# An attention recurrence and two MoE layers on one core: where the first weights are decoded, and in which order the first two units start

## The chip, the cores and the metric

The kernel runs on one core of one Trainium2 chip. The metric is device time in microseconds (us) of one execution; each timed number is the median of several runs. The core has five engines with queues of their own, each working its queue in order: TensorE (PE; PEld is its weight load), VectorE (DVE), ScalarE (ACT), GpSimd (POOL), and SyncE (SP), which here issues all DMAs.

## The reference

Attention with a complex decay, then two layers on its output. What is computed, cut to what matters:

```python
scale = np.minimum(mag, 0.999) / (mag + 1e-06)          # mag = |a|
a_re_n, a_im_n = a_re * scale, a_im * scale
for t in range(S):                                      # per batch, head: S is D x D
    S_re, S_im = ar * S_re - ai * S_im + k_t v_t, ar * S_im + ai * S_re
    y[:, :, t] = q_t @ S_re
x = y.transpose(0, 2, 1, 3).reshape(B * S, H * D)
x = (silu(x @ w_gate) * (x @ w_val)) @ w_out
h = x @ w_in
return (h - np.tanh(h)) @ w2_out
```

Four batches, 8 heads, 768 positions, head size 48: 3072 tokens of 384 values. The first layer has 1536 inner columns, the second 2048. The weights come as float64, q, k, v and a as float32.

## The kernel before

**Attention.** A unit is 128 positions of one batch, all heads (24 units); a group is two units. `group_steps` makes the decay's weights for a group: normalise a (`squares`, `norm_root`, `norm`), transpose it on TensorE and copy it into `PL` (`put_a`), then 14 cumulative complex products on VectorE (`cstep`: one product of 128x384 into `prod`, L266, and two sums back into `PL`, L268 and L269), seven along e and seven along b. Between the products of group 0 stands the normalisation of group 1. Then `PL` is copied to `NW` (L312, L313), its inverse is made (two squares L345 and L346, root L348, square L349, products L347, L350, L351), and the factors over the unit's length go out to `lam_d` and come back as `LS`. `PL` has one buffer, so group 1's copies wait for group 0's `NW`.

`unit_a` transposes a unit's q and k (`psQ`), multiplies with the weights to `QK` (L370, L371, L376), writes `QK` to HBM and reads it back with heads apart as `TK` and `TQ` (L378, L383), and transposes k's part (`psK`). `unit_b` makes scores (`psS`, L420), masks them, makes the state `Z` (`psG`), its shifted copy `Zs` through a DMA, and on GpSimd `Hn` from the earlier state (L413 to L415); then the output `psY`, its copy `y` (L450), and the transposed token block `x` in two parts, cast and residual (L463, L464). `QK`, `TK`, `Kn` and `Z` have one buffer, `TQ` has two. `window(b, a)` interleaves the steps of one unit's `unit_b` with the next one's `unit_a`.

**MoE 1.** `moe1_tile` works on 2 or 3 units of tokens (`TILES`). For each of 12 blocks of inner columns it makes 18 matmuls (`l`, L554), Silu on ScalarE (L558), the gated product on VectorE (L563), a split into cast and residual (L514, L515) and nine matmuls with the output weights (`acc`, L538). Between these steps `bg` draws steps of attention for later tiles. MoE 2 follows after the last tile.

**Decode.** A weight block arrives as raw 64-bit words. `words` makes a float32 of it in one pass on ScalarE (L140) and four on VectorE (L141 to L144); `decode` splits it into a cast (L150) and a residual, the latter on TensorE (L158 to L160) if `by_pe`, or on VectorE (L152). `dec1_jobs` is a list of 24: the gate and value columns of blocks 0 to 7 ("gv", 128x768), then in turn an output block ("o", 128x384) and a gate and value block. `raw` has two buffers, and `dec1` loads the next block only behind the decode that frees a buffer. `dec1(3)` is called while group 0 is made; `dec1(N_PRE + 2)`, up to the tenth job, after the code of units 0 and 1, and `bg` in the first tile makes the rest.

**Order.** The kernel is written as these streams, and a scheduler then puts the instructions into each engine's queue: in the order of the code by priority, with later code moved ahead where an engine would wait by its own reckoning. `tc.issue_after(ins)` makes the instructions in its block, on the engine of `ins`, stand behind `ins`; it is no wait.

Of the kernel before, what the change touches and what calls it, by code (L numbers as in the profile page):

```python
# [13 lines left out]
ALU = mybir.AluOpType  # L14
# [27 lines left out]
def tile_kernel(ctx: ExitStack, tc: tile.TileContext, q, k, v, a_re, a_im, w_gate, w_val, w_out, w2_in, w2_out, out):  # L42
    nc = tc.nc
    PE, ACT, DVE, POOL, SP = nc.tensor, nc.scalar, nc.vector, nc.gpsimd, nc.sync
# [17 lines left out]
    N_PRE, QAT, QDEP = 8, 15, 4  # L62
# [121 lines left out]
    def dec1(n, by_pe=False):  # L184
        while prog["dec"] < min(n, len(dec1_jobs)):
            kind, f = dec1_jobs[prog["dec"]]
            r = raws[prog["dec"]]
            prog["dec"] += 1
            t = raw_p.tile([P, 2 * DM], F32, tag="dt", name="dt", bufs=2)
            if kind == "o":  # L190

                w = m1.tile([P, 2, DM], F32R, tag="wo", name="wo", bufs=3)
                wo_t[f] = w
                decode(r[:, 0], w[:, 0], w[:, 1], t[:, 0:DM])
                SP.dma_start(out=wo_d[f], in_=w.bitcast(F32))
            else:
                decode(r.rearrange("p a c -> p (a c)"), *wgv[f], t, by_pe)
            dec1_load()
# [18 lines left out]
    def load_qkv(u):  # L217
        if u < NU:
            for nm, src in (("q", q), ("k", k), ("v", v)):
                t = a2.tile([P, DM], F32, tag=nm, name=nm)  # L220
                SP.dma_start(out=heads(t), in_=nat(src, u))
                st[nm, u] = t

    def squares(eng):
        ar, ai = st["a"]
        s1, s2 = T("s1"), T("s2")
        ACT.activation(out=s1, in_=ar, func=AF.Square)
        ACT.activation(out=s2, in_=ai, func=AF.Square)
        eng.tensor_tensor(out=s1, in0=s1, in1=s2, op=ALU.add)
        st["sq"] = s1, s2  # L230
# [31 lines left out]
    def cstep(prev, cur, n):  # L262

        sh = [P, 2] + list(cur.shape[1:])
        pr = a2.tile(sh, F32, tag="prod", name="prod", bufs=1)
        DVE.tensor_tensor(out=pr, in0=prev.unsqueeze(2).to_broadcast(sh), in1=cur.unsqueeze(1).to_broadcast(sh), op=ALU.mult)  # L266
        cv, pv = cur.rearrange("p (n c) r -> p n c r", n=n), pr.rearrange("p i (n c) r -> p i n c r", n=n)
        DVE.tensor_tensor(out=cv[:, :, 0], in0=pv[:, 0, :, 0], in1=pv[:, 1, :, 1], op=ALU.subtract)  # L268
        DVE.tensor_tensor(out=cv[:, :, 1], in0=pv[:, 0, :, 1], in1=pv[:, 1, :, 0], op=ALU.add)  # L269

    def group_steps(g0):
        grp = list(range(g0, g0 + G))
# [24 lines left out]
                yield  # L297
        rows = PL.rearrange("p e c b g j h -> p (e c) b (g j h)")
        for b in range(1, 8):
            cstep(rows[:, 14:16, b - 1], rows[:, :, b], 8)  # L300
            yield
            if g0 == 0 and b == NA0:
                squares(DVE)
                norm_root(G)
                yield
                norm(DVE)
                yield
# [157 lines left out]
        yield  # L465

    def window(b, a):

        b = unit_b(b) if b is not None else iter(())
        a = unit_a(a) if a is not None else iter(())  # L470

        for s_ in (a, b, b, a, a, b, a, b, a, b):
            if next(s_, 0) is None:
                yield
        for s_ in (b, a):
            for _ in s_:
                yield
# [180 lines left out]
    prog = {"done": -1, "n": 0, "dec": 0, "credit": 0.0, "group": 0, "unit": -1, "more": 0.0}  # L658
# [23 lines left out]
    while prog["done"] < TILES[0] - 1:  # L682
        att_next(TILES[0] - 1, SHARE0)
        if prog["n"] == QAT:

            dec1(QDEP - 1, True)
            for u in range(2):
                with tc.issue_after(raw_ins[QDEP]):
                    load_qkv(u)
    dec1(N_PRE + 2, True)  # L690
    banks[:] = [(ps_a, "at")]
    second = ExitStack()
    w2_hl, w2 = [], []
# [64 lines left out]
    with tc.If(bad > 0):  # L758
        with ExitStack() as gen:
# [12 lines left out]
            with tc.For_i(0, q.shape[2], TB) as t0:  # L772
# [24 lines left out]
                for t in range(TB):  # L797
                    rows = [x[:, t, :].unsqueeze(2).to_broadcast(full) for x in (ar, ai, qq, kk)]
# [102 lines left out]
```

## Time and profile before

| what | us |
|---|---|
| median of 3 runs (lowest to highest) | 1247.72 (1244.65 to 1250.12) |
| the profiled execution | 1244.15 |
| its span, first to last instruction | 1242.4 |
| TensorE busy, share of the span | 1131.6, 91% |
| VectorE busy | 989.9, 80% |
| ScalarE busy | 693.9, 56% |
| start of the first tile's first matmul | 129.9 |

The profile is of one execution. A line of its timeline says when an instruction started and how long it took, which line of the kernel it comes from, and, in brackets, how long its engine had been idle and what ended that. Matmul ends are modelled, so a busy TensorE is not at its peak. The granted clock is the share of full speed that TensorE was given: 0.5 is 1.2 GHz, 1.0 is 2.4 GHz.

### The profile page before, as it was taken

To read this page: it belongs to the slowest core of one execution; us is meant where nothing else is said; L and a number is where in the kernel's file an instruction comes from. 1 tells how busy PE (TensorE), PEld (TensorE's weight loads), DVE (VectorE), ACT (ScalarE), POOL (GpSimd) and SP (SyncE) were. 2 spreads that over 40 slices of the span, in tenths; PEclk is the share of its full clock that TensorE was granted. 3 is DMA by queue.
4 is the path that set the end of the run, shared out by engine and by line. 5 is a ranking of instruction groups with operands and counts; after the bars stand their busy time and mean duration, and the time that the engine had idled before them with its cause. 6 is when DMAs were issued, how large, how long until landed. Compare 5 with 4: busy or idle time off the path is not lost.

```text
span 1242.4 us, 20766 instructions
## 1 busy us (share of the span) xinstructions
PE 1131.6 (91%) x7512; PEld 1100.3 (89%) x7512; DVE 989.9 (80%) x2255; ACT 693.9 (56%) x1454; POOL 124.2 (10%) x108
## 2 busy tenths in 40 slices
PE   4337898999899999999999999989999999999997
PEld 2116898999899899999999999988999999999997
DVE  6988897797796859687684428899898898898986
ACT  6463847657556363746535225566666656566664
POOL 0002241231120102122011000000000000000000
PEclk9656899999999999999999999989999999999999
DMA  6585668688777687768755538860110101101000
GB/s 172 145 194 160 160 194 192 170 205 199 179 184 193 163 204 175 167 140 196 181 139 137 164 97 258 264 206 33 58 33 26 58 1 58 39 20 58 1 20 22
DMA packets 282286, 163.50 MB, mean 132 GB/s; under 512 B 155328, under 2 KB 263232, under 8 KB 282176
## 3 DMA queue, kind: packets, MB, share of 16 engines
q1 hardware_dynamic: 282176, 162.10, 50.3%
q8 instruction: 61, 1.00, 0.3%
q14 instruction: 49, 0.40, 0.1%
HBM read 121.26 MB, written 37.86 MB: 128 GB/s over the span
## 4 chain that ended last, share of the span: by engine, by line
PE 62%; DVE 15%; ACT 12%; DMA 8%; issue 2%; SPq 1%; ACTq 0%; DVEq 0%
PE l L635 15%; PE l L617 15%; PE l L554 15%; PE acc L538 7%; PE psS L420 3%; DMA TQ<-qk_d 2%; DVE prod L266 2%; DMA qk_d<-QK 1%; DVE PL L268 1%; ACT NW L313 1%; PE psY L448 1%; DVE lo L515 1%; PE psY L446 1%; DVE QK L376 1%; DMA raw<-in_moe_w_val_dram 1%
## 5 line engine op out<-in xcount | busy, mean ns | idle before, releaser
L554 PE MATMUL l<-x,wgv 128*128 128x256 f32 (+1 forms) x2160 | 361.4, 313 | 11.6 <-ACT t L558 7.5
L554 PEld LDWEIGHTS l<-x,wgv 128*128 128x128 f32 x2160 | 320.6, 194 | 14.9 <-ACT t L558 8.7
L635 PE MATMUL l<-x,wi 128*128 128x384 f32 x1152 | 223.1, 338 | 6.3 <-DVE t L584 5.7
L635 PEld LDWEIGHTS l<-x,wi 128*128 128x128 f32 x1152 | 202.4, 189 | 8.4 <-DVE t L584 7.4
L514 ACT CAST hi<-t 128x384 fp32r<-128x384 f32 (+1 forms) x248 | 119.0, 480 | 154.0 <-DVE t L563 125.3
L617 PE MATMUL l<-w,hi 128*128 128x384 f32 x768 | 178.4, 338 | 0.0
L538 PE MATMUL acc<-hi,wo 128*128 128x256 f32 (+1 forms) x720 | 175.8, 309 | 0.6 <-DMA wo<-wo_d 0.6
L515 DVE TENSOR_TENSOR lo<-t,hi 128x384 fp32r<-128x384 f32 (+1 forms) x248 | 138.0, 556 | 32.2 <-ACT hi L514 31.8
L617 PEld LDWEIGHTS l<-w,hi 128*128 128x128 f32 x768 | 139.1, 189 | 0.0
L577 ACT ACTIVATE t<-l 128x384 f32<-128x384 f32 x128 | 63.4, 496 | 125.1 <-PE l L635 110.0
L538 PEld LDWEIGHTS acc<-hi,wo 128*128 128x128 f32 x720 | 125.0, 191 | 0.9 <-issue 0.8
L538 PE MATMUL acc<-lo,wo 128*128 128x256 f32 (+1 forms) x360 | 109.6, 310 | 1.8 <-DVE lo L515 1.6
L617 PE MATMUL l<-w,lo 128*128 128x384 f32 x384 | 110.4, 337 | 0.0
L563 DVE TENSOR_TENSOR t<-t,l 128x256 f32<-128x256 f32 (+1 forms) x120 | 56.2, 469 | 60.0 <-PE l L554 43.4
L266 DVE TENSOR_TENSOR prod<-PL 128x384 f32<-128x384 f32 x168 | 100.1, 596 | 2.9
L579 DVE TENSOR_TENSOR l<-l,t 128x384 f32<-128x384 f32 x128 | 72.2, 564 | 35.4 <-ACT uu L578 34.3
L558 ACT ACTIVATE t<-l 128x256 f32<-128x256 f32 (+1 forms) x120 | 51.6, 430 | 63.0 <-PE l L554 62.3
L580 ACT ACTIVATE vv<-uu,gbias 128x384 f32<-128x384 f32 x128 | 80.0, 625 | 2.8
L420 PE MATMUL psS<-TQ,TK 96*128 96x128 f32 x384 | 55.9, 296 | 27.1 <-DMA TQ<-qk_d 25.7
L420 PEld LDWEIGHTS psS<-TQ,TK 96*128 96x128 f32 x384 | 52.1, 209 | 29.0 <-issue 21.8
L584 DVE COPY_PREDICATED t<-far,l 128x384 f32<-128x384 int32 x128 | 75.7, 592 | 2.5
L538 PEld LDWEIGHTS acc<-lo,wo 128*128 128x128 f32 x360 | 68.7, 191 | 2.7 <-DVE lo L515 2.7
(130 smaller groups left out, 1856.4 us busy)
## 6 DMA issues: line engine op xcount, KB each, us to landing
wo<-wo_d SPq DMA_DIRECT2D x108, 384.0 KB, 3.9
qk_d<-QK SPq DMA_DIRECT2D x24, 768.0 KB, 4.7
raw<-in_moe_w_out_dram SPq DMA_DIRECT2D x28, 384.0 KB, 3.3
TK<-qk_d SPq DMA_DIRECT2D x48, 192.0 KB, 4.0
TQ<-qk_d SPq DMA_DIRECT2D x48, 192.0 KB, 5.0
x<-o_d SPq DMA_DIRECT2D x16, 576.0 KB, 5.2
raw<-in_moe_w_in_dram SPq DMA_DIRECT2D x16, 384.0 KB, 4.1
ar<-in_a_re_dram SPq DMA_DIRECT2D x24, 192.0 KB, 4.1
```

The costliest lines, as they stand in the source:

```text
L266: DVE.tensor_tensor(out=pr, in0=prev.unsqueeze(2).to_broadcast(sh), in1=cur.unsqueeze(1).to_broadcast(sh), op=ALU.mult)
L420: PE.matmul(ps[:, P * i:P * (i + 1)], lhsT=TK[:, 4 * hh + i], rhs=TQ[:, 4 * hh + i], start=True, stop=True)
L514: ACT.copy(out=hi, in_=t)
L515: DVE.tensor_tensor(out=lo, in0=t, in1=hi.bitcast(F32), op=ALU.subtract)
L538: PE.matmul(acc[j], lhsT=w[:, a, j * P:(j + 1) * P], rhs=m[b], start=(f == 0 and i == 0), stop=(f == NF1 - 1 and i == 2))
L554: PE.matmul(p, lhsT=w[a][:, kk], rhs=x[b][:, kk, 0:n_t], start=(n == 0), stop=(n == 3 * NJ - 1))
L577: ACT.activation(out=t, in_=p, func=AF.Tanh)
L579: DVE.tensor_tensor(out=p, in0=p, in1=t, op=ALU.subtract)
L580: ACT.activation(out=vv, in_=uu, func=AF.Square, scale=1.0 / G_C, bias=gbias)
L584: DVE.copy_predicated(out=t, mask=far, data=p)
L617: PE.matmul(acc[tb], lhsT=g[a][:, tb * P:(tb + 1) * P], rhs=w2_hl[f][:, b], start=(f == 0 and n == 0), stop=(f == NF2 - 1 and n == 2))
L635: PE.matmul(p, lhsT=wi_hl[a][:, kk, sl], rhs=x[b][:, kk, :], start=(n == 0), stop=(n == 3 * NJ - 1))
```

## The change

Two things are changed. The decode of jobs 3 to 9 (called by `dec1(N_PRE + 2, True)`) is put into a block `issue_after` on the last sum of group 0's last product, kept in `prog["cs"]`: on VectorE none of its passes may stand ahead of that sum. And `window`, for the pair of unit 0's `unit_b` and unit 1's `unit_a`, takes three steps of unit 1 first (queries, keys, `QK` and its DMAs), then five of unit 0, then the last two of unit 1.

```diff
@@ cstep
-        DVE.tensor_tensor(out=cv[:, :, 1], in0=pv[:, 0, :, 1], in1=pv[:, 1, :, 0], op=ALU.add)
+        return DVE.tensor_tensor(out=cv[:, :, 1], in0=pv[:, 0, :, 1], in1=pv[:, 1, :, 0], op=ALU.add)
@@ group_steps
         for b in range(1, 8):
-            cstep(rows[:, 14:16, b - 1], rows[:, :, b], 8)
+            cs = cstep(rows[:, 14:16, b - 1], rows[:, :, b], 8)
+            if g0 == 0:
+                prog["cs"] = cs.ins
@@ window
+        first = a == 1
...
-        for s_ in (a, b, b, a, a, b, a, b, a, b):
+        for s_ in (a, a, a, b, b, b, b, b, a, a) if first else (a, b, b, a, a, b, a, b, a, b):
@@ main
-    dec1(N_PRE + 2, True)
+
+    with tc.issue_after(prog["cs"]):
+        dec1(N_PRE + 2, True)
```

Line numbers behind the first edit grow by two, and by up to five towards the end: L383 becomes L385, L558 becomes L561. The queues change as follows. In the names, `dt_687`, `dt_705`, `dt_723`, `dt_741` are the decodes of blocks 3 to 6, `dt_954` is block 9's, `dt_776`, `dt_886` and `dt_1048` are those of output blocks 0 to 2; `raw_738` is block 7's raw weights, `raw_756` output block 0's, `raw_803` block 9's.

VectorE before, in the later half of group 0's products, with group 1's normalisation (L248 to L250):

```order
L266 TENSOR_TENSOR prod_330<-PL_160 128x384
L248 TENSOR_TENSOR s1_245<-s1_245,s2_246 128x768
L141 TENSOR_SCALAR dt_723<-dt_723 128x768
L268 TENSOR_TENSOR PL_160<-prod_330 128x8x12
L269 TENSOR_TENSOR PL_160<-prod_330 128x8x12
L249 SCALAR_TENSOR_TENSOR ai_208<-ai_208,sgn_69,s1_245 128x768
L250 TENSOR_TENSOR ar_205<-ar_205,s1_245 128x768
L142 TENSOR_SCALAR dt_723<-dt_723 128x768
L266 TENSOR_TENSOR prod_334<-PL_160 128x384
L141 TENSOR_SCALAR dt_741<-dt_741 128x768
L143 SCALAR_TENSOR_TENSOR dt_723<-raw_702,dt_723 128x768
```

VectorE now, from the last but one of group 0's products on:

```order
L266 TENSOR_TENSOR prod_342<-PL_160 128x384
L268 TENSOR_TENSOR PL_160<-prod_342 128x8x12
L269 TENSOR_TENSOR PL_160<-prod_342 128x8x12
L266 TENSOR_TENSOR prod_346<-PL_160 128x384
L268 TENSOR_TENSOR PL_160<-prod_346 128x8x12
L269 TENSOR_TENSOR PL_160<-prod_346 128x8x12
L141 TENSOR_SCALAR dt_687<-dt_687 128x768
L141 TENSOR_SCALAR dt_705<-dt_705 128x768
```

The decodes of blocks 4 to 6 no longer stand between the products; those of blocks 3 and 4 begin behind the last sum, and the others later still.

SyncE before, from unit 0's `QK` to its `TQ` and the store behind it:

```order
L378 DMA qk_d_85<-QK_414 128x12x128
L177 DMA raw_896<-in_moe_w_out_dram 128x384
L221 DMA q_662<-in_q_dram 128x8x48
L383 DMA TK_418<-qk_d_85 48x8x128 x2
L383 DMA TQ_419<-qk_d_85 48x8x128 x2
L195 DMA wo_d_83<-wo_887 128x768
```

SyncE now, from unit 0's `QK` to unit 1's `TK`:

```order
L380 DMA qk_d_85<-QK_414 128x12x128
L221 DMA q_662<-in_q_dram 128x8x48
L221 DMA k_664<-in_k_dram 128x8x48
L180 DMA raw_738<-in_moe_w_gate_dram 128x3x128
L385 DMA TK_418<-qk_d_85 48x8x128 x2
L385 DMA TQ_419<-qk_d_85 48x8x128 x2
L180 DMA raw_738<-in_moe_w_val_dram 128x3x128
L380 DMA qk_d_85<-QK_482 128x12x128
L177 DMA raw_756<-in_moe_w_out_dram 128x384
L385 DMA TQ_487<-qk_d_85 48x8x128 x2
L385 DMA TK_486<-qk_d_85 48x8x128 x2
```

A load of raw weights (block 7) now stands ahead of unit 0's `TK`, and unit 1's `QK` and `TQ` follow unit 0's directly, with its `TK`, which waits for the one buffer, last.

ScalarE before, ahead of the first Silu (`t_816`):

```order
L348 ACTIVATE x2_840<-NW_682,tiny_78 128x768
L259 COPY PL_1125<-psA_1157 128x3x8x8 x2
L260 COPY A0_1126<-psA_1157 128x3
L349 ACTIVATE x2_840,chk_82<-x2_840 128x768
L558 ACT_TABLE_LOAD
L558 ACTIVATE t_816<-l1_806 128x256
```

ScalarE now, at the same place:

```order
L140 ACTIVATE dt_954<-raw_803 128x768
L348 ACTIVATE x2_840<-NW_682 128x768
L259 COPY PL_1125<-psA_1127 128x3x8x8 x2
L260 COPY A0_1126<-psA_1127 128x3
L140 ACTIVATE dt_1048<-raw_896 128x384
L561 ACT_TABLE_LOAD
L561 ACTIVATE t_816<-l1_806 128x256
L259 COPY PL_1125<-psA_1157 128x3x8x8 x2
L260 COPY A0_1126<-psA_1157 128x3
L350 ACT_TABLE_LOAD
L350 ACTIVATE x2_840<-NW_682,tiny_78 128x768
L561 ACT_TABLE_LOAD
L561 ACTIVATE t_952<-l1_942 128x256
```

The first passes of block 9 and of output block 2 stand ahead of the first Silu, and group 1's root (L350, before L348) behind it, with a table load on either side.

## Rows read from the trace of the kernel before

**Rows 1.** Windows: stretch, length; busy PE, PEld, DVE, ACT, POOL; clock; DMA, GB/s.

```profile
0.00:129.90 129.90, 61.07 (x230) 42.52 (x230) 104.03 (x222) 68.15 (x129) 12.70 (x21) 0.69 0.64 164
...
129.90:261.20 131.30, 121.46 (x989) 119.24 (x987) 109.39 (x267) 83.98 (x180) 34.94 (x25) 0.96 0.77 190
...
160.00:180.00 20.00, 17.77 (x145) 17.59 (x144) 20.00 (x44) 7.66 (x17) 12.60 (x6) 0.91 0.73 203
```

**Rows 2.** Timeline (start, length in us, engine, line): group 0's last sum.

```profile
58.31 0.25 DVE L269 TENSOR_TENSOR PL<-prod 128x96 f32<-128x96 f32 x1
```

**Rows 3.** Timeline, from group 0's products to unit 0's QK.

```profile
62.00 0.89 ACT L313 COPY NW<-PL 128x384 f32<-128x384 f32 x1
...
67.27 0.83 ACT L259 COPY PL<-psA 128x192 f32<-128x192 f32 x2 [0.32 <-PE psA L256]
...
79.91 0.95 DVE L376 TENSOR_TENSOR QK<-qk,NW 128x768 f32<-128x768 f32 x1
```

**Rows 4.** Timeline, unit 0's QK through HBM to its scores.

```profile
80.89 0.37 SPq L378 DMA_DIRECT2D qk_d<-QK  x1
...
86.23 1.16 SPq L383 DMA_DIRECT2D TQ<-qk_d  x2
...
93.13 3.75 PE L420 MATMUL psS<-TQ,TK 96*128 96x128 f32 x16 [11.01 <-DMA TQ<-qk_d]
```

**Rows 5.** Timeline, unit 0's output, unit 1, the first gated product.

```profile
98.39 1.95 PE L446 MATMUL psY<-v,SC 128*128 128x48 f32 x16
...
102.45 1.59 DVE L376 TENSOR_TENSOR QK<-qk,NW 128x768 f32<-128x768 f32 x1
...
114.38 3.76 PE L420 MATMUL psS<-TQ,TK 96*128 96x128 f32 x16 [5.38 <-DMA TQ<-qk_d]
...
127.34 0.46 ACT L450 COPY y<-psY 128x384 f32<-128x384 f32 x1
...
132.17 1.28 ACT L558 ACT_TABLE_LOAD   x1
...
135.31 0.41 DVE L563 TENSOR_TENSOR t<-t,l 128x256 f32<-128x256 f32 x1
```

**Rows 6.** Timeline, two first decode passes; DMA issues, median us to landing.

```profile
43.25 0.90 ACT L140 ACTIVATE dt<-raw 128x768 f32<-128x768 f32 x1 [0.72 <-DMA raw<-in_moe_w_val_dram]
...
117.01 0.92 ACT L140 ACTIVATE dt<-raw 128x768 f32<-128x768 f32 x1
...
raw<-in_moe_w_val_dram SPq DMA_DIRECT2D x12, 384.0 KB, 4.9
```

**Rows 7.** VectorE's groups up to 129.9 us: busy us, mean ns | idle.

```profile
L144 DVE SCALAR_TENSOR_TENSOR dt<-raw,dt 128x768 int32<-128x768 int32 x12 | 11.4, 949 | 0.1
...
L141 DVE TENSOR_SCALAR dt<-dt 128x768 f32<-128x768 f32 x12 | 6.8, 564 | 7.3 <-ACT dt L140 7.3
...
L144 DVE SCALAR_TENSOR_TENSOR dt<-raw,dt 128x384 int32<-128x384 int32 x5 | 2.7, 549 | 0.0
...
L141 DVE TENSOR_SCALAR dt<-dt 128x384 f32<-128x384 f32 x5 | 1.8, 355 | 4.1 <-ACT dt L140 4.1
```

**Rows 8.** VectorE's waits from 129.9 to 261.2 us: total, times, longest.

```profile
DVE t L563 <- PE l L554: 6.7, 6, 2.7
DVE NW L347 <- ACT x L346: 3.4, 2, 2.3
```

**Rows 9.** Timeline, last output block's decode; the second tile's fifth gated product.

```profile
193.31 1.06 DVE L152 TENSOR_TENSOR wo<-dt,wo 128x384 fp32r<-128x384 f32 x1 [2.05 <-ACT wo L150]
...
217.31 0.41 DVE L563 TENSOR_TENSOR t<-t,l 128x256 f32<-128x256 f32 x1
```

**Rows 10.** Timeline, GpSimd beside VectorE.

```profile
98.57 2.10 POOL L250 TENSOR_TENSOR ar<-ar,s 128x768 f32<-128x768 f32 x1
...
98.93 1.85 DVE L268 TENSOR_TENSOR PL<-prod 128x96 f32<-128x96 f32 x1
...
163.29 6.32 POOL L414 TENSOR_TENSOR Zs<-Zs,LS 96x384 f32<-96x384 f32 x1 [8.91 <-DMA Zs<-Z]
```

## The prediction

> **What bounds the kernel now.** I read the stages first. Up to 129.9 us, where the first matmul of the first MoE tile starts, TensorE is busy for less than half of the time at a mean granted clock of 0.69; VectorE is busy for 104.03 us. In the next two tiles TensorE is busy for 121.46 of 131.3 us [rows 1]. So the start is a chain of waits, and from there on time is TensorE's. A start that ends earlier reaches the end as it is, unless the two tiles behind it become longer. The forecast is the sum of these two.
>
> The chain of the start, in order of time: group 0's cumulative products on VectorE, which end at 58.56 [rows 2]; the rest of that group's weights, and unit 0's QK, whose second pass ends at 80.86 [rows 3]; QK through HBM into TK and TQ, and unit 0's scores at 93.13 [rows 4]; unit 1's QK at 104.04, its scores at 114.38, its y at 127.34, the load of Silu's table at 132.17 and the first gated product (L563) at 135.31 [rows 5]. I take that product as the end of the start, since TensorE's third block can't be written before it frees a bank.
>
> **Term 1: group 0's products.** Before, the decodes of blocks 4, 5 and 6 stand among them (block 3's was done ahead of them). One decode is two passes of 0.56 us and two of 0.95 [rows 7], 3.0 us, or 2.7 since neighbours overlap by some 0.09. Three are 8.0 us; I take 0.5 off for gaps between products that they filled. Group 0 ends at 58.56 - 7.5 = 51.0. The price: block 5's raw weights can be loaded only when block 3's last pass has freed their buffer, and that pass now stands behind the products, with block 4's between its passes: four long ones, four short ones and the group's small joins put it at 57.6.
>
> **Term 2: unit 0's QK.** ScalarE has four copies and two squares to make, at 0.78 us a piece (a copy is 0.89 long and overlaps its successor [rows 3]): 51.0 to 55.7. Then its order puts two sets of evictions of group 1 (0.83 and a small copy each [rows 3]) ahead of the root, and block 3's cast and half a set ahead of the root's square, which ends at 61.5. Two VectorE passes of 0.95 end at 63.3. The cast and copies ahead of qk's second half end at 65.6, and two QK passes at 67.5. Before it was 80.86: 13.3 us earlier.
>
> **Term 3: the scores.** On SyncE the load of block 7 now stands ahead of TK, and it waits for block 5's decode. That one's own load is issued by 61.6 and takes 4.9 us to land [rows 6]; its passes, between qk and products, end at 72.9. QK has landed by then: it is issued at 80.89 and read by 86.23 at the latest [rows 4], so 67.5 + 5.3. TK and TQ go out from 73.4, TQ at 74.5, and from TQ's issue to the scores it took 6.9 us [rows 4]: 81.4. TensorE has block 6's products ahead of the scores until 82.0. Unit 0's scores: 82.0 against 93.13. Unit 1's QK no longer stands behind them: its transposes follow unit 0's, and it ends at 75.5 against 104.04 [rows 5]. But TK has one buffer. Unit 1's TK waits for unit 0's last score, 82.0 + 3.8 [rows 4], and lands some 5 us later: scores at 91 against 114.38. That is the reordering's gain at its largest, 23 us.
>
> **Term 4: from there to the first gated product.** Some is handed back. Between unit 1's scores and its y TensorE now has block 7's decode, group 2's first transposes and the state's product. Half of unit 1's output, 16 matmuls, takes 1.95 us at the rate of 98.39 [rows 5] and twice that at the lower clock (0.69 on average over the start): y at 102 to 110 against 127.34. What decides then is a load. ScalarE has the first decode pass of an output block ahead of the first Silu; that block's load stands on SyncE behind block 9's, which waits for block 8's last pass at 108 to 113.5 (block 8's own load stood behind that of v, which unit 0's output freed at 94). Load 4.9, two first passes and two sets of evictions 3.5, table 1.28 [rows 5], Silu 0.4: the first gated product at 118 to 124. I take 121.5. **At the start: 135.3 - 121.5 = 13.8 us gained.**
>
> **Term 5: what is put off.** Ahead of the first gated product VectorE has 28 instructions fewer: 12 long ones of decode (four of 0.56, eight of 0.95 with three residuals), 12 short ones (five of 0.35, seven of 0.55), and two long passes (0.95) and two halves of qk (0.35) of group and unit. By the durations [rows 7] that is 18.1 us, and 15.7 without the overlaps. At the third tile's first gated product both orders have done the same work. So these two tiles carry 15.7 us more on VectorE: 109.39 + 15.7 = 125.1. Of its idle 21.9 us, 6.7 are waits for TensorE [rows 8], which a fuller engine need not make; the other twelve lines of waits, from the 3.4 us for ScalarE's squares down [rows 8], are 12.5 together and stay. 125.1 + 12.5 = 137.6 against 131.3: **6.3 us handed back**, between 0 (all idle time is filled) and 15.7 (none is). Two further table loads, since Silu and the root alternate at the tile's start, are 2.6 us of ScalarE, counted at nothing: it is busy for 83.98 of 131.3 us [rows 1]. Without that cover they cost 2.6.
>
> **Sum.** -13.8 + 6.3 = -7.5 us. The profiled execution took 1244.15 us (span 1242.4), which gives 1236.6; it lies 3.6 under the median of the runs, 1247.72. Against the median: 1240.2. What the measurement can tell from no change is about 0.5%, 6.2 us.
>
> **Rivals.** *Hidden whole.* VectorE fills its idle time, which is 21.9 us against the 15.7 put off, and the start alone counts: 13.8 us, or up to 17 with the full clock in term 4: 1231 to 1234. Against it: from 160 to 180 VectorE has no idle time at all [rows 1], and this is where blocks 9 to 11 now fall.
>
> *All handed back.* VectorE and GpSimd shut each other out: a 128x96 pass, 0.25 elsewhere, took 1.85 us while GpSimd had a product running, and one of GpSimd's took 6.32 us beside a full VectorE [rows 10]. Then VectorE's idle time beside GpSimd's 34.94 us [rows 1] isn't free, nothing fits in, and all of term 5 comes back: -13.8 + 15.7 = +1.9, 1249.6. The Trainium skill, "SBUF — State Buffer", section "SBUF: two separate sides", says that the port pair which the two share is an exclusive lock, held for an instruction, while the other blocks; by that rule the time would be this rival's. The trace agrees on the lock, with the 1.85 us, but in the 6.32 us it was GpSimd that was kept out, so deferred passes can also push GpSimd's work aside.
>
> *Decode too slow, and the kernel slower.* The raw weights have two buffers, so blocks go in rounds of two: load, first pass, three passes, next load. Before, one buffer's first passes start at 43.25 and, five rounds later, at 117.01 [rows 6]: 14.8 us a round. In the first tile seven output blocks end within 45.3 us, the last residual starting at 193.31 [rows 9]: 15.1 us for two. Now some twelve blocks, six rounds, are left behind the first gated product. TensorE's order needs the last ahead of the second tile's sixth block, about at its fifth gated product, 82 us on (217.31 [rows 9]), with term 5 some 88. At 14.8 six rounds end at 89, just in time. It decides from (88 + 7.5) / 6 = 15.9 us a round, and each us above costs six: at 17, 1247.7 + 6.5 = 1254.
>
> *It doesn't do what it says.* If the decodes had stood behind the products in any case, queueing them would move nothing; the order shows that three stood among them, so this gets no chance.
>
> **Chances.** Forecast (3 to 13 us faster) 0.47, hidden whole 0.15, all handed back 0.22, decode too slow 0.16. Faster by over 0.5%, under 1241.5: 0.31 of the forecast's and all of the hidden, 0.46. Within 0.5%: 0.16 of the forecast's, all of the handed back and 0.03 of the last, 0.41. Slower: 0.13. The range goes from the hidden case with the higher clock, 1230, to rounds of 17 us, 1255; the likeliest case's own is 1235 to 1245.
>
> **What the changed profile would show.** Group 0's last product near 51 (term 1); unit 0's QK near 67.5 (2); unit 0's scores near 82 and unit 1's near 91 (3); the first gated product at 118 to 124, with ScalarE waiting for a raw load ahead of its Silu (4); VectorE busy for over 90% of two tiles, and the third tile's start, 261.2 before [rows 1], some 7 us earlier (5). The forecast is wrong if a landing or SyncE's order holds unit 1's scores beyond 100, or if the first two tiles grow by more than 14 us.

## The result and the profile after

| what | us |
|---|---|
| before, median of 11 runs (lowest to highest) | 1245.54 (1242.24 to 1250.12) |
| after, median of 11 runs (lowest to highest of the 10 compared) | 1255.93 (1251.38 to 1258.66) |
| after : before | 1.0078, 95% interval 1.0062 to 1.0094 |
| the profiled execution of after, its span | 1256.67, 1254.9 |

The change makes the kernel 0.8% slower; 1240.2 was forecast, and 1255.93 lies just beyond the range's upper end of 1255. One of the 11 executions after took 2235.31 us and is left out of the range and the ratio. A second measurement of the same kernel (e12 below) gave 1.0091 (1.0058 to 1.0124).

The start first. Timeline of the kernel after (start, length in us, engine, line): group 0's last sum, QK of units 0 and 1, scores of units 0 and 1, unit 1's y, a copy of group 1's weights, a first decode pass, the load of Silu's table, the first gated product.

```profile
49.19 0.25 DVE L269 TENSOR_TENSOR PL<-prod 128x96 f32<-128x96 f32 x1
...
62.87 1.82 DVE L378 TENSOR_TENSOR QK<-qk,NW 128x768 f32<-128x768 f32 x2
...
73.35 2.85 DVE L378 TENSOR_TENSOR QK<-qk,NW 128x768 f32<-128x768 f32 x2 [0.99 <-ACT wgv L150]
...
81.72 2.46 PE L422 MATMUL psS<-TQ,TK 96*128 96x128 f32 x16 [0.30 <-DMA TQ<-qk_d]
...
90.64 2.05 PE L422 MATMUL psS<-TQ,TK 96*128 96x128 f32 x8
...
105.14 0.48 ACT L452 COPY y<-psY 128x384 f32<-128x384 f32 x1 [2.72 <-PE psY L450]
...
110.94 0.85 ACT L314 COPY NW<-PL 128x384 f32<-128x384 f32 x1 [1.06 <-DVE PL L268]
...
117.65 0.57 ACT L140 ACTIVATE dt<-raw 128x384 f32<-128x384 f32 x1
...
118.24 1.28 ACT L561 ACT_TABLE_LOAD   x1
...
119.95 0.42 DVE L566 TENSOR_TENSOR t<-t,l 128x256 f32<-128x256 f32 x1 [0.42 <-ACT t L561]
```

These are the lines that answer to [rows 2 to 5], and they stand where the prediction put them: group 0 at 49.4 (51.0 was said), unit 0's QK at 64.7 (67.5), its scores at 81.7 (82.0), unit 1's at 90.6 (91), its y at 105.1 (102 to 110), the first gated product at 119.95 (121.5) against 135.31. The start is 15.3 us shorter. Its last link is another than was told: the two first decode passes ahead of the first Silu waited for no load. ScalarE last waited at 110.94, for group 1's last sum on VectorE, and then worked without a gap to the table load at 118.24.

Then the whole execution, cut at four products of L563/L566: the first, the 25th (third tile), the 73rd (seventh tile) and the last one (120th). First before, then after; columns as in [rows 1].

```profile
0.00:135.30 135.30, 66.46 (x256) 47.61 (x257) 107.73 (x227) 72.22 (x137) 16.47 (x24) 0.68 0.64 163
135.30:265.90 130.60, 120.63 (x998) 118.51 (x998) 110.35 (x274) 84.11 (x181) 31.18 (x23) 0.97 0.78 196
265.90:527.70 261.80, 245.50 (x2047) 241.10 (x2045) 201.18 (x487) 148.71 (x318) 47.05 (x38) 0.98 0.75 180
527.70:822.10 294.40, 292.08 (x1904) 288.51 (x1905) 201.99 (x463) 133.84 (x269) 29.53 (x24) 0.99 0.66 177
822.10:1242.40 420.30, 406.93 (x2313) 404.59 (x2311) 368.61 (x809) 255.02 (x552) 0.00 (x0) 0.99 0.12 40
```

```profile
0.00:120.00 120.00, 56.73 (x251) 40.95 (x251) 91.31 (x200) 64.70 (x123) 11.16 (x21) 0.76 0.63 154
120.00:270.10 150.10, 130.47 (x992) 125.58 (x993) 125.58 (x300) 93.97 (x196) 35.58 (x25) 0.91 0.76 197
270.10:536.20 266.10, 250.06 (x2043) 247.07 (x2043) 198.23 (x488) 147.02 (x315) 53.39 (x38) 0.95 0.73 176
536.20:834.40 298.20, 295.60 (x1920) 292.41 (x1919) 203.74 (x463) 135.64 (x272) 28.09 (x24) 0.98 0.65 174
834.40:1254.90 420.50, 407.32 (x2313) 405.09 (x2311) 368.96 (x809) 255.99 (x552) 0.00 (x0) 0.99 0.12 39
```

The first two tiles (second line) take 150.1 us instead of 130.6: 19.5 us against a gain of 15.3, and the third tile starts 4.2 us later than before. Of the 19.5, TensorE's idle time is 9.7 (19.6 against 10.0, length less busy time) and its busy time 9.8 (130.47 against 120.63), with six matmuls fewer: the granted clock is 0.91 instead of 0.97, so more of the same matmuls ran at 1.2 GHz. The next four tiles lose 4.3 us more: there idle time is the same (16.0 and 16.3), the matmuls are the same to four, and busy time is 4.6 longer at a clock of 0.95 instead of 0.98. The four tiles behind them lose 3.8. From there on both are alike. So of the 12.5 us by which the profiled span grew, 4.2 are there at the third tile's start and 8.3 come behind it.

A second profile of each (e15 and e12) shows which of this belongs to the kernel. The second and third stretch again, first of before, then of after:

```profile
136.20:266.80 130.60, 120.15 (x998) 118.04 (x998) 111.10 (x274) 84.03 (x181) 30.44 (x23) 0.97 0.78 199
266.80:527.90 261.10, 244.18 (x2047) 239.47 (x2045) 201.40 (x486) 148.51 (x318) 46.86 (x38) 0.99 0.74 180
```

```profile
119.80:272.60 152.80, 131.74 (x993) 126.89 (x994) 125.22 (x299) 93.92 (x196) 31.94 (x25) 0.91 0.76 194
272.60:541.90 269.30, 252.49 (x2041) 248.70 (x2040) 199.87 (x489) 147.47 (x315) 50.08 (x38) 0.94 0.71 174
```

Both repeat: 130.6 us twice for before, 150.1 and 152.8 for after; the clock 0.97 twice, 0.91 twice. What the fourth stretch loses (294.4 and 294.8, 298.2 and 297.7) repeats in length, but not in kind: in the second execution it is idle time.

Where does the third tile's start come from? Timeline of before: last sums of groups 1 and 2, the residual of unit 5's tokens, and the third tile's first matmul.

```profile
122.98 0.25 DVE L269 TENSOR_TENSOR PL<-prod 128x96 f32<-128x96 f32 x1
...
182.81 0.24 DVE L269 TENSOR_TENSOR PL<-prod 128x96 f32<-128x96 f32 x1
...
261.23 0.56 DVE L464 TENSOR_TENSOR x<-psX,x 128x384 fp32r<-128x384 f32 x1 [1.26 <-ACT x L463]
...
261.25 0.50 PE L554 MATMUL l<-x,wgv 128*128 128x256 f32 x2 [0.39 <-ACT x L463]
```

And of after, with the load of the third tile's first weights, which waits for the cast of those tokens, and TensorE's wait for the residual right behind it:

```profile
110.82 0.25 DVE L269 TENSOR_TENSOR PL<-prod 128x96 f32<-128x96 f32 x1
...
187.91 0.25 DVE L269 TENSOR_TENSOR PL<-prod 128x96 f32<-128x96 f32 x1
...
262.55 0.50 PEld L557 LDWEIGHTS l<-x,wgv 128*128 128x128 f32 x2 [0.30 <-ACT x L465]
...
264.52 0.55 DVE L466 TENSOR_TENSOR x<-psX,x 128x384 fp32r<-128x384 f32 x1
...
265.12 0.90 PE L369 MATMUL psQ<-ident,q 128*128 128x128 f32 x3 [1.78 <-DVE x L466]
```

In both the third tile starts when unit 5's tokens are there, and in before the trace said so in the bracket at 261.25. There the wait was only 0.39 us, so TensorE's own work was nearly as late; in after it was 0.30 and 1.78. Group 1's weights came 12.2 us earlier, but group 2's, from which unit 5 is made, 5.1 later, and unit 5 3.3 later. Between the two groups VectorE did more decode. The decode's own instructions (the tile `dt`), before, from group 0 to 1 and from 1 to 2; columns PE, PEld, DVE, ACT, clock, DMA, GB/s:

```profile
58.60:123.20 64.60, 7.94 (x12) 2.48 (x10) 27.91 (x42) 12.35 (x17) 0.61 0.67 170
123.20:183.10 59.90, 0.00 (x0) 0.00 (x0) 18.66 (x36) 7.45 (x14) 0.88 0.68 177
```

The same of after:

```profile
49.40:111.10 61.70, 14.29 (x24) 6.01 (x24) 22.80 (x34) 10.66 (x14) 0.73 0.68 162
111.10:188.20 77.10, 0.00 (x0) 0.00 (x0) 30.05 (x52) 12.95 (x21) 0.89 0.65 176
```

That is 11.4 us more decode from group 1 to group 2. VectorE waited there too (engine, line, what for: us in total, times, longest), before and then after:

```profile
DVE dt L141 <- ACT dt L140: 2.2, 1, 2.2
DVE NW L350 <- ACT x L349: 1.6, 1, 1.6
```

```profile
DVE dt L141 <- ACT dt L140: 6.4, 3, 4.1
DVE NW L352 <- ACT x L351: 3.3, 1, 3.3
DVE s L244 <- ACT s L236: 2.3, 1, 2.3
```

VectorE works its queue in order, so a decode pass that waits for its raw weights' first pass on ScalarE holds group 2's products behind it. The longest of these waits, 4.1 us, ends at 116.37: it lies ahead of the first gated product, and there it was ScalarE's queue that came late, not the load.

The same for the two tiles as a whole, from the first to the 25th gated product, VectorE and then TensorE. Before:

```profile
DVE t L563 <- PE l L554: 6.7, 6, 2.7
DVE dt L141 <- ACT dt L140: 0.8, 1, 0.8
PE l L554 <- ACT t L558: 2.1, 2, 1.1
```

After:

```profile
DVE dt L141 <- ACT dt L140: 6.2, 4, 2.2
DVE PL L287 <- ACT A L260: 3.5, 1, 3.5
DVE lo L518 <- ACT hi L517: 2.9, 2, 2.7
PE l L557 <- ACT t L561: 7.0, 6, 3.0
PE psA L256 <- ACT A L260: 3.7, 2, 2.5
```

VectorE's wait for TensorE went, as forecast (6.7 to nothing; 4.9 to 3.3 in the second pair of profiles). All its waits for ScalarE together rose from 10.7 to 23.3 us (12.0 and 23.2 in the second pair), and TensorE's from 2.5 to 11.5 (3.8 and 13.7). ScalarE was busy for 9.9 us more (93.97 against 84.11): the moved blocks' first passes and casts are its work too, and it loaded tables twice more. It was not full, though, and its own first passes waited for 10.5 us, 5.2 of them for loads and the rest for VectorE. That points to the order of queues that wait for each other more than to ScalarE's load; it is argued, and no run tests it by itself.

### The profile page after: what moved, and what is told of

Same layout as the page of the kernel before. It is cut to its first block, busy times and chain, and to the rows that moved or that the text cites. A ratio compares the mean times of both kernels' runs of the same rounds, so it can differ in the third digit from the quotient of the medians.

```text
span 1254.9 us, 20795 instructions
## 1 busy us (share of the span) xinstructions
PE 1140.2 (91%) x7512; PEld 1111.1 (89%) x7512; DVE 987.8 (79%) x2255; ACT 697.3 (56%) x1456; POOL 128.2 (10%) x108
## 4 chain that ended last, share of the span: by engine, by line
PE 63%; DVE 13%; ACT 10%; DMA 9%; issue 3%; SPq 2%; POOL 0%; ACTq 0%; DVEq 0%
PE l L557 16%; PE l L620 15%; PE l L638 15%; PE acc L541 8%; PE psS L422 3%; DMA qk_d<-QK 2%; DVE prod L266 2%; DMA ar<-in_a_re_dram 2%; PE psY L448 2%; PE psY L450 2%; DVE PL L268 1%; PE psG L434 1%; PE psA L256 1%; ACT L561 1%; DMA TQ<-qk_d 1%
## 5 line engine op out<-in xcount | busy, mean ns | idle before, releaser
L557 PE MATMUL l<-x,wgv 128*128 128x256 f32 (+1 forms) x2160 | 370.6, 320 | 18.3 <-ACT t L561 13.0
L557 PEld LDWEIGHTS l<-x,wgv 128*128 128x128 f32 x2160 | 330.5, 201 | 23.2 <-ACT t L561 16.8
L518 DVE TENSOR_TENSOR lo<-t,hi 128x384 fp32r<-128x384 f32 (+1 forms) x248 | 131.4, 531 | 33.2 <-ACT hi L517 32.9
L566 DVE TENSOR_TENSOR t<-t,l 128x256 f32<-128x256 f32 (+1 forms) x120 | 56.2, 468 | 65.4 <-PE l L557 37.2
L266 DVE TENSOR_TENSOR prod<-PL 128x384 f32<-128x384 f32 x168 | 103.7, 617 | 2.7
L561 ACT ACTIVATE t<-l 128x256 f32<-128x256 f32 (+1 forms) x120 | 51.4, 428 | 83.6 <-PE l L557 79.4
L586 DVE SCALAR_TENSOR_TENSOR t<-vv,t 128x384 f32<-128x384 f32 x128 | 70.5, 551 | 0.8
L620 PEld LDWEIGHTS l<-w,lo 128*128 128x128 f32 x384 | 70.9, 189 | 0.3 <-DVE lo L518 0.3
L448 PE MATMUL psY<-v,SC 128*128 128x48 f32 x384 | 70.5, 277 | 0.0
```

What stands on the lines that cost most here:

```text
L448: PE.matmul(o, lhsT=SC[h // 4][:, h % 4], rhs=vn[:, D * h:D * (h + 1)], start=True, stop=(c == 0))
L518: DVE.tensor_tensor(out=lo, in0=t, in1=hi.bitcast(F32), op=ALU.subtract)
L557: PE.matmul(p, lhsT=w[a][:, kk], rhs=x[b][:, kk, 0:n_t], start=(n == 0), stop=(n == 3 * NJ - 1))
L586: DVE.scalar_tensor_tensor(out=t, in0=vv, scalar=G_F, in1=t, op0=ALU.add, op1=ALU.mult)
L620: PE.matmul(acc[tb], lhsT=g[a][:, tb * P:(tb + 1) * P], rhs=w2_hl[f][:, b], start=(f == 0 and n == 0), stop=(f == NF2 - 1 and n == 2))
```

## The experiments

Sixteen runs, all ratios to the kernel before on the same chip.

| run | what is run | us | ratio (95%) |
|---|---|---|---|
| e1 | decode behind the last product, old order of units | 1246.46 | 0.9984 (0.9964 to 1.0003) |
| e16 | decode behind the 11th product, old order | 1246.62 | 1.0024 (1.0004 to 1.0043) |
| e2 | decode as before, new order of units | 1257.41 | 1.0077 (1.0050 to 1.0105) |
| e4 | decode behind the 8th product, new order | 1260.88 | 1.0103 (1.0073 to 1.0133) |
| e3 | decode behind the 11th product, new order | 1247.36 | 1.0003 (0.9984 to 1.0022) |
| e12 | the whole change again | 1258.75 | 1.0091 (1.0058 to 1.0124) |
| e15 | before again | 1245.42 | 1.0002 (0.9985 to 1.0019) |
| e5 | whole change, fewer decode passes | 1244.43 | 1.0006 (0.9980 to 1.0032) |
| e6 | before, fewer decode passes | 1240.15 | 0.9953 (0.9924 to 0.9982) |
| e7 | whole change, raw weights in halves | 1257.17 | 1.0103 (1.0045 to 1.0161) |
| e8 | before, raw weights in halves | 1254.83 | 1.0080 (1.0051 to 1.0110) |
| e9 | e2, first tile held back | 1255.24 | 1.0062 (1.0039 to 1.0085) |
| e10 | whole change, first tile held back | 1251.10 | 1.0019 (0.9998 to 1.0040) |
| e11 | e3, first tile held back | 1254.27 | 1.0062 (1.0039 to 1.0086) |
| e13 | before, third to tenth tile freed of attention | 1250.56 | 1.0033 (1.0012 to 1.0054) |
| e14 | whole change, freed likewise | 1249.68 | 1.0046 (1.0022 to 1.0070) |

**One part alone, and the decode's place (e1 to e4, e16).** e1 takes back the new order, e2 the queueing; e3, e4 and e16 queue the decode behind an earlier product of group 0.

```diff
@@ e1
-        for s_ in (a, a, a, b, b, b, b, b, a, a) if first else (a, b, b, a, a, b, a, b, a, b):
+        for s_ in (a, b, b, a, a, b, a, b, a, b):
@@ e2
-    with tc.issue_after(prog["cs"]):
-        dec1(N_PRE + 2, True)
+    dec1(N_PRE + 2, True)
@@ e3 (e4: b == 1; e16: as e3, with the order of e1)
-            if g0 == 0:
+            if g0 == 0 and b == 4:
                 prog["cs"] = cs.ins
```

> Only the decode is queued behind group 0's products; unit 0 and unit 1 start in the old order. In VectorE's order 9 instructions fewer than before stand ahead of the first gated product (28 fewer in the whole change), among them one decode of a gate and value block and one of an output block. Theory A (what is put off in VectorE's queue comes back in the first two tiles with a surcharge: the whole change put off 15.7 us and lost 19.5): the first gated product some 4 to 7 us earlier than 135.3, the 25th no earlier than before, total within 4 us of before, 1243 to 1250. Theory B (the new order of the two units is what costs, the decode's place is the gain): total 8 us or more under before. Theory C (what is lost later, in the fifth tile, is an accident of the order that any edit brings): the first three tiles as in A, but a loss of some 8 us in a single later tile here too.

> Only the order of units 0 and 1 is changed; the decode stands where it stood. Ahead of the first gated product VectorE has 22 instructions fewer, but of the decode only one output block (four short passes and a residual, 2.2 us) is among them. Theory A: the first gated product 8 to 14 us earlier than 135.3, some 4 us of it handed back by the 25th, total 4 to 9 us under before, 1237 to 1242. Theory B: the first two tiles grow by more than the start gains, total 5 us or more over before. Theory C: as A up to the third tile, and a loss of some 8 us in one later tile, total 1245 to 1250.

> The whole change, but the decode is queued behind the eleventh of group 0's fourteen products and not behind the last. Ahead of the first gated product stand one gate and value block and one output block fewer than before (in the whole change two and three). Theory A: the start gains less than the whole change's 15.5 us, 9 to 12, but hands back less, some 8 to 10; total 1241 to 1247, 8 to 14 under the whole change. Theory B: the same total as the whole change, since the order of the units is the same. Theory C: first two tiles as in A, later loss of its own.

> The whole change, but the decode is queued behind the eighth of group 0's fourteen products (the first along b). Ahead of the first gated product only one output block's decode fewer than before. Theory A: close to the kernel with the new order of the units alone, 4 to 9 us under before, 1237 to 1243. Theory B: over before, like the whole change. Theory C: first three tiles as in A, later loss of its own.

Theory A was my first: what VectorE puts off comes back. It was right on e1's third tile (first gated product at 267.5) and total, though e1's start gained 2.1 us and not 4 to 7, and e3's total lies 0.4 us beyond its bounds; but it was wrong on e2 and e4, which put off least of the decode and lose most. The first gated product came 2.1 (e1), 8.4 (e2), 13.3 (e3) and 5.9 (e4) us earlier than the 135.3 of before, the 25th at 267.5, 270.2, 267.8 and 286.6: later than 265.9 in every one. No gain of the start, of any size, got as far as the third tile. Theory B, the new order as the cause, fits e2 and e4 but not e3, with the same order and no loss. The two parts don't add up: the order costs 0.8% with the decode where it was, 1.0% with it behind the 8th product, nothing behind the 11th. Theory C has no support either: the fifth tile is long in after and e2 (69.2 and 70.3 us against 59.8 before), but tiles three to six together take 266.1 (after), 265.9 (e1), 268.7 (e2), 262.8 (e3) and 262.0 (e4) against 261.8, so of what one tile loses others give back a part, and 4 to 7 us stay lost in after, e1 and e2.

> The old order of the units, the decode queued behind the eleventh of group 0's products. Theory A: units 0 and 1 gain some 4 us, group 2 ends no earlier than 183, total 1243 to 1249, the same as before. Theory L: as the decode is put off less than with the last product (1246.5), 1243 to 1246.

With the old order the decode's place does little: first gated product at 131.8, the 25th at 268.6, total within 0.25% of before, as theory A of that expectation (the third tile waits for unit 5) has it.

**Less work on VectorE (e5, e6).** Two of the four decode passes are left out from the eleventh job on, and the weights with them are not right.

```diff
...
+        if less:
+            DVE.scalar_tensor_tensor(out=ti, in0=w[:, :, 0], scalar=29, in1=ti, op0=ALU.logical_shift_right, op1=ALU.bitwise_or)
+            return
...
```

> The whole change, with two of the four VectorE passes of the decode left out for every job from the eleventh on (three gate and value blocks, eleven output blocks), so those weights are wrong; loads, first passes, casts and residuals stay. That takes 3 x (0.56 + 0.95) + 11 x (0.35 + 0.55) = 14.4 us of VectorE out of the first tile and the time just ahead of it. Theory V (VectorE's queue up to the last product of group 2 sets the third tile's start; what starts earlier only changes places in that queue, and what differs between orders is VectorE's idle time): the third tile's first gated product at 256 to 260 against 270.1, total 1241 to 1247. Theory X (the serial chain of the attention units, their trips through HBM, sets the third tile's start whatever VectorE does): still 267 to 270, total 1252 to 1257. Theory W (what costs is the wait for raw weights in their two buffers): the passes left out shorten each round by 1 to 1.5 us, 263 to 267, total 1248 to 1253.

> The kernel before with the same 14.4 us of VectorE passes left out (two of four decode passes from the eleventh job on). V: the third tile's first gated product at 253 to 258 against 265.9, total 1234 to 1240, and still no later than the same cut in the whole change. X: 264 to 267, total 1244 to 1249. W: 260 to 264, total 1240 to 1245.

The changed kernel gains 11.5 us (1244.43 against 1255.93) from 14.4 us of passes, the kernel before 5.2 from the same. In e5 group 2's last sum starts at 183.8 instead of 187.9, unit 5's residual at 261.1 instead of 264.5, and the 25th gated product is at 265.3: 5 us later than V's bounds and where W had it, while the total is V's. In e6 group 2 is 4.5 us earlier than before, but unit 5 is not (260.9), and the 25th product comes at 269.0, later than all three theories had it; V fails there. By the ratios the gains are 0.7% and 0.5%, and their intervals overlap: that a deferred pass costs more than the same pass in its old place is likely, but not shown. Group 2's weights don't set the third tile's start in every order. And VectorE's idle time in e5's first two tiles is 25.7 us (144.10 less 118.36), no less than in after: fewer passes did not shorten its waits.

**Raw weights in halves (e7, e8).** Four buffers of half the size, a load and a decode for each half.

```diff
...
-    RAW, MID = 2, 3
+    RAW, MID = 4, 3
-            r = raw_p.tile([P, 2, DM], I64, tag="raw", name="raw", bufs=RAW)
+            r = raw_p.tile([P, DM], I64, tag="raw", name="raw", bufs=RAW)
...
```

> The whole change, with the raw weights loaded and decoded in halves of 128x384 (gate and value apart) in four buffers of half the size: the same bytes of buffer, but a load starts as soon as half a block is done, and four output blocks fit instead of two. VectorE's decode grows by 12 x (2 x 1.80 - 3.02) = 7 us. W: the rounds of two go, VectorE's idle time between the last products of groups 1 and 2 falls from 12.2 to under 7 us, and the third tile's first gated product comes at 262 to 267, total 1246 to 1252. V: VectorE has more to do, and that product comes at 272 to 278, total 1257 to 1264.

> The kernel before with the raw weights loaded and decoded in halves in four half-sized buffers. W: 2 to 5 us under before, 1242 to 1246. V: VectorE has 7 us more to do ahead of the third tile; 5 to 8 us over before, 1252 to 1256.

W's sign came, its time did not: VectorE's wait for first passes is gone between groups 1 and 2 (60.23 us busy of 66.2), yet e7 takes 1257.17, with its third tile at 282.2, later than both theories had it. e8 is slower by what V said. The halves cost 0.8% in the kernel before and 0.25% in the changed one, but e7's interval (0.45 to 1.61% over before) is too wide to say whether the buffers are worth something there. What the two runs show is that freer buffers, bought with 7 us more work on VectorE, don't bring the third tile forward. The prediction's rival "decode too slow", whose number (1254) is the nearest, is answered by the kernel after itself: its last residual of a decode ends at 206.6, and the second tile's fifth gated product, at which it was to be needed, comes at 208.6; TensorE waits for no decode there. It was in time, if by 2 us only.

**Holding the first tile back (e9 to e11).** The first gated product is queued behind the last product of group 1's inverse.

```diff
...
-            DVE.tensor_tensor(out=s, in0=s, in1=ps[1], op=ALU.mult)
+            with tc.issue_after(prog["w2"]) if ti == 0 and f == 0 else ExitStack():
+                DVE.tensor_tensor(out=s, in0=s, in1=ps[1], op=ALU.mult)
```

> The new order of the two units alone (decode where it stood), and the first gated product queued on VectorE behind the last product of group 1's inverse; in the run without that queueing it stood 38 instructions ahead of it. Theory H (the earlier first tile only overtakes the weights of groups 1 and 2, which the second and third tile need; the first tile's Silu, casts and products then stand in ScalarE's and VectorE's queues ahead of them, and both wait for each other): first gated product 5 to 9 us later than 126.9, last product of group 2 at 186 to 190 against 196.5, the third tile's first gated product 264 to 267, total 1246 to 1250 against 1257.4. Rival K (the order of units 0 and 1 costs by itself, through their DMAs and buffers): the start's gain is lost and group 2 still ends at 195 or later, total 1256 to 1264.

> The whole change with the first gated product queued behind the last product of group 1's inverse (it stood 8 instructions ahead of it). H: little moves at the start, first gated product 125 to 129, but the first tile's blocks then crowd group 2 (two more of them stand ahead of its last product): third tile 264 to 270, total 1249 to 1256. K: as the whole change, 1254 to 1258.

> Decode queued behind the eleventh of group 0's products, the new order of units, and the first gated product queued behind group 1's inverse (it stood 28 instructions ahead). H: group 2 ends 3 to 6 us earlier than the 190.9 without that queueing, third tile 262 to 266, total 1240 to 1246. K: 1247 or later.

H fell, on e9 and e11, and K's bounds miss e9 as well (1255.24, with group 2 early). In e9 group 2 ended as H said, but unit 5 did not follow. Timeline of e9: group 2's last sum (196.24 in e2) and unit 5's residual (264.81 in e2).

```profile
189.76 0.25 DVE L269 TENSOR_TENSOR PL<-prod 128x96 f32<-128x96 f32 x1
...
268.67 0.55 DVE L468 TENSOR_TENSOR x<-psX,x 128x384 fp32r<-128x384 f32 x1
```

e11 is worse than e3 by 0.6%, against H too. But e10 is worth a look: its first gated product comes 6.2 us later than in the whole change (126.2), and it is 0.6 to 0.7% faster. The first tile's start by itself is not worth what the prediction gave it.

**The second profiles (e12, e15).**

> The changed kernel once more, for a second profile. If the 41 us more at the lower clock in the ten tiles (61.7 against 20.4) belong to the kernel, a second execution shows 45 to 75 us of them again, most ahead of the seventh tile, and the third tile's first gated product within 3 us of 270.1. If they belong to one execution, under 40 us.

> The kernel before once more, for a second profile. If the difference of the two profiles is the kernels' and not that of single executions: third tile's first gated product within 3 us of 265.9, 15 to 30 us at the lower clock in the ten tiles (20.4 in the first profile, against 61.7 and 58.0 in the two of the changed kernel).

Both came as the first reading has it (above): the third tile's first gated product at 272.6 and 266.8, and 58.0 and 20.5 us at the lower clock in the ten tiles.

**Freeing the later tiles of attention (e13, e14).** From the third tile on the first layer reads a slice of weights instead of the tokens, so no tile waits for a unit, and the output is not the reference's.

```diff
-                    PE.matmul(p, lhsT=w[a][:, kk], rhs=x[b][:, kk, 0:n_t], start=(n == 0), stop=(n == 3 * NJ - 1))
+                    PE.matmul(p, lhsT=w[a][:, kk], rhs=x[b][:, kk, 0:n_t] if ti < 2 else wgv[0][b][:, kk:kk + n_t // P], start=(n == 0), stop=(n == 3 * NJ - 1))
```

> The kernel before, with the first layer of the third to tenth tile multiplying a slice of the weights of block 0 in place of the tokens, so these tiles wait for no attention unit (their outputs are wrong; the number and sizes of the matmuls stay). Before, TensorE is busy for 120.6 of the 130.6 us from the first to the 25th gated product, so little can move: 25th gated product at 262 to 267 by theory A and by L, total 1239 to 1248.

> The whole change, with the third to tenth tile freed of the attention units in the same way. Theory A (the third tile waits for unit 5, which is no earlier than before): the 25th gated product at 252 to 262 against 270.1 and 272.6, TensorE's clock between the first and the 25th at 0.94 or more against 0.91, total 1240 to 1248, no more than 2 us over the same cut in the kernel before. Theory L (too much work in the first two tiles): 266 to 272, total 1252 to 1259.

Timeline of e14: the 25th gated product, and behind it unit 5's residual.

```profile
258.08 0.41 DVE L566 TENSOR_TENSOR t<-t,l 128x256 f32<-128x256 f32 x1
...
267.48 0.55 DVE L466 TENSOR_TENSOR x<-psX,x 128x384 fp32r<-128x384 f32 x1
```

Its first two tiles, columns as in [rows 1]:

```profile
117.80:258.10 140.30, 122.26 (x963) 117.95 (x963) 115.54 (x280) 85.94 (x186) 31.03 (x24) 0.95 0.75 191
```

Unit 5 is as late as in the kernel after, but the third tile no longer waits for it and starts 12 us earlier, with a clock of 0.95 instead of 0.91. In e13, whose order still has unit 5's residual ahead, that product is at 269.3, later than expected. The changed kernel's handicap goes: 1249.68 against 1250.56. (Both totals lie above what I expected; the stretch behind the last gated product takes 427 us in both instead of 420.)

This shows that in the changed kernel unit 5 holds the third tile back. It doesn't show that the wait itself is the price. Of the 9.8 us by which the two tiles are shorter than in after, 1.6 are idle time (18.0 us left of 19.6) and 8.2 busy time: 29 matmuls fewer, which stand behind now, and a higher clock. In after the clock was 0.60 from 253.3 to 270.1, ahead of the third tile's product; in e14 it was 1.00 from 165.3 to 258.1. Nor does the early third tile reach the end: its lead over e13, 11.2 us, is 1.2 at the seventh tile (527.45 against 528.68), with the moved matmuls in between.

## Why the prediction was wrong, point by point

- **Terms 1 to 4** (the start) held in their dates: 15.3 us gained, 13.8 forecast, every date within 3 us. The mechanism was as told up to unit 1's y. The last link was not: "what decides then is a load", with "ScalarE waiting for a raw load ahead of its Silu". ScalarE waited for no load there, but for group 1's last sum (110.94), and then worked off its queue. That 119.95 came so near 121.5 is in part luck.
- **Term 5** is the step that failed. Its load was right: VectorE was to be busy for 15.7 us more in the two tiles, and was for 15.2 (125.58 against 110.35). Its idle time was not. The step let 21.9 us shrink to 12.5; it measured 24.5 (150.1 less 125.6). The 6.7 us of waits for TensorE, "which a fuller engine need not make", did go. What was said to "stay" at 12.5 did not: the waits for ScalarE, 10.7 us before, became 23.3. (A further 2.7 us, 21.9 less 6.7 less 12.5, were dropped without a reason.) Handed back were 19.5 us, not 6.3, and more than the bound of 15.7, at which no idle time is filled. The bound left out that what is moved can wait itself, and that it moves ScalarE's work with it: decode passes waited 6.2 us for first passes against 0.8, and the two further table loads, "counted at nothing", were only 2.6 of ScalarE's 9.9 us. With TensorE's own waits for ScalarE, 2.5 us before and 11.5 after, this is where the idle time of the two tiles grew.
- **The frame of the sum** was wrong as well: "the forecast is the sum of these two", start and load. The third tile starts when unit 5 is there. A step that dated unit 5 (group 1's weights, group 2's, the unit) as carefully as units 0 and 1 were dated would have asked what the 15.7 us do to group 2, and found part of them ahead of it: 11.4 us more decode, and all twelve of the first tile's gated products instead of nine.
- **What the sum had no term for** is TensorE's clock behind the start, and tiles three to ten. In the first two tiles 9.7 us more idle time came with 9.8 us more busy time, at a clock of 0.91 against 0.97 in both pairs of profiles. The Trainium skill, "TensorE: Matmul & The Clock Gate", section "HAM oscillation — how this bites in real kernels", tells of a kernel whose TensorE waits for a DMA in every round and starts each next round at the lower clock, so that its waits cost more than their length; the trace agrees in kind, but e14, with 18.0 us idle at 0.95, shows that the sum of the waits doesn't set the price. Tiles three to six lost 4.3 and 8.2 us in the two pairs, where idle time was the same and busy time 4.6 and 8.3 longer. Of the 20.0 us between the forecast for the profiled execution (1236.6) and its time (1256.67), term 5 is 13.2, the start -1.5, and what lies behind the third tile's start 8.3.
- **Its test** named the case: wrong "if the first two tiles grow by more than 14 us". They grew by 19.5.
- **The rivals.** *All handed back* was near in kind (15.7 us against 19.5), but 6.3 us short in time (1249.6). Its mechanism, VectorE and GpSimd shutting each other out, was not tried; the traces show no sign of more of it, since VectorE's passes were not longer (15.2 us more busy where 15.7 were counted) and none of its listed waits in the two tiles of after is for GpSimd. *Decode too slow* was not the cause: the decode was in time. *Hidden whole* is excluded.
- **The reordering**, the largest gain of the prediction ("23 us" at unit 1's scores), did bring unit 1 forward by 23.7 us (90.64 against 114.38) and, made alone, costs 0.8%.
- **Open**: why the new order alone (e2) is slow. In e2 the last product of group 1's inverse starts 11.3 us later than before (144.5 against 133.2), and the first tile overtakes it; but queueing the tile behind it (e9) took 0.8% to 0.6%, which the intervals don't separate. Nor is it settled why e3, with the decode behind the 11th product, escapes, though TensorE waits for ScalarE there as long as in after (12.4 us in its first two tiles), nor why 8.3 us are lost behind the third tile's start. That the lower clock in tiles three to six follows from what went before, and not the other way round, is argued from e14's second stretch, not shown for those tiles.

## What to carry to other kernels

Where a pipeline feeds tiles, date the feeding chain up to the tile that is known to wait, not only the first output of the start; the bracket at a tile's first matmul says who it waits for, but not the price: here it was 2.1 us of wait, and 12 us went when the tile was freed. When work moves, move it on every engine that has a part in it: here VectorE's passes were counted, and ScalarE's first passes and casts were not. Work that is moved behind a chain on an in-order queue lands ahead of the next chain, and takes its own waits along, so idle time on that engine is no cover unless the moved instructions' inputs are there. Two reorderings need not add up (0.8% and nothing alone, 0.8% together, nothing with another place for one of them): run the parts and the places.

## What the runs showed of the hardware

In the first two tiles 9.7 us more idle time of TensorE came with 9.8 us more busy time, for 992 matmuls instead of 998. It is similar in the slowest order (e4): 157.2 us there instead of 130.6, of which 14.6 are busy time (135.26 against 120.63, 998 matmuls in each) and 12.0 idle, at a clock of 0.89. But there is no fixed price: e14 has 18.0 us idle, 8.0 more than before, and was busy for 1.6 us more, with 35 matmuls fewer, at 0.95. In the kernels before and after the clock belongs to the order, not to the execution: the clocks of the two pairs of profiles agree to 0.01 in every stretch from the first gated product to the 73rd.
